# Attention and two MLPs on one core: the first chunk's output in two parts, and where weight conversions stand

## The chip, the cores and the metric

One core of a Trainium2 chip runs the whole program. The metric is the device time of one execution in microseconds; of the kernel before, three timed runs gave 955.28 to 957.27 with a median of 955.95.

## The reference

Attention with local and global queries, and then two MLPs, all in float32 (the weights arrive as float64):

```python
# q_l, k_l, v_l: (4, 8, 512, 64)   q_g, k_g, v_g: (4, 8, 32, 64)
k_all, v_all = concat([k_g, k_l]), concat([v_g, v_l])
out_g = softmax(q_g @ k_all.T / 8) @ v_all
s_ll  = where(abs(i - j) <= 32, q_l @ k_l.T / 8, -1e9)
out_l = softmax(concat([q_l @ k_g.T / 8, s_ll])) @ v_all
x = concat([out_g, out_l])  ->  (2176 tokens, 512)
h = x @ w_in;  x = max(0.01 h, h) @ w_out       # first MLP, 512 -> 2048 -> 512
h = x @ w2_in; out = (h - tanh(h)) @ w2_out     # second MLP, same sizes
```

## The kernel before

**Precision.** Every float32 matrix of an MLP is split into two parts (`hi` and `lo`, tiles of type F32R), and a product is three matmuls: hi*hi, lo*hi, hi*lo. Weights arrive as pairs of 32-bit words. `convert_w` (L117) makes float32 of them with one ScalarE step (L126) and three VectorE steps on integers (L127, L131, L134); `split_w` (L139) then makes hi on ScalarE and lo on VectorE. A conversion in this text is all six steps for one 128-wide slice of a weight matrix.

**Chunks and items.** The 2176 tokens are cut into five chunks of 512, 512, 512, 256 and 384 (the last with the 128 global tokens). The hidden size of 2048 is 16 slices f of 128. An item (phase, c, f) is one slice of one chunk. In phase 1 an item does `mlp1_a(c, f)`, 12 matmuls that make h, and the ScalarE and VectorE steps that make g, its hi part gh and its lo part gl; two items later (`SKEW`) `mlp1_b(c, f)` does 12 matmuls that add this slice's share to the chunk's y in four PSUM banks y0 to y3. After f = 15 `mlp1_y` (L226) copies the four banks out and stores them to `y_dram[c]`. All 16 slices of chunk 0 come first, then those of chunk 1, and so on; item number n = 16 c + f. Phase 2 is the second MLP, over the same chunks.

**Attention.** `stage(s)` (L762) returns up to five operations for one pair of heads and half a batch row (32 pairs): keys and queries of s + 1 by transposition (`kps`, `qps`), scores of s (`sps`) and their softmax, the output of s - 2 (`avps`) with the global scores (`sgps`), and the two transpositions of the probabilities of s - 1 (`ptps`). Global queries add `gtps`, `gt2ps` and `gavps` now and then. A chunk can start when the stages that fill its x have run: stages up to 17 for chunk 1, 25 for chunk 2, 33 for chunks 3 and 4.

**Order.** Stages 0 to 9 (`PRE` = 10) run ahead of the first item, with seven PSUM banks to rotate through (`start_tags`, L752); later attention has three (`run_tags`), while h has one bank and y four. Then the table `beside` (L861 to L872) says which operations go with which item: stages 10 to 17 beside items 0 to 15, 18 to 25 beside 15 to 31, 26 to 33 beside 31 to 47. They are put between the item's eight steps. TensorE's order is as written for items 0 to 77 (`fix`, L820); the other engines' order, SP's queue of transfers among them, is made by the planner from a simulation and the order of the code.

**Weights of the first MLP.** `in_load` (L682) loads a slice of w_in, 512 KB; `in_job` (L699) converts it in place, and it stays. One load stands ahead of the stages, one in each of the ten stages, and one in each of the first items; one conversion stands in each of stages 2 to 9 (eight), the other eight in items 0 to 7. `out_job` converts a slice of w_out, in items 1 to 16, and stores both parts to DRAM; later chunks fetch them (`wo_fetch`, L154), two items ahead. A conversion of these is kept behind the latest exponential and the latest attention output in the code (`converted`, L693).

**Weights of the second MLP.** From item 22 to 44 `w2_job` (L725) converts the 32 slices and stores them to DRAM, through two buffers `wraw` for loads and two `wf` for converted tiles; chunk 4's items fetch them.

**Places of x.** `xh` and `xl` are two pairs of tiles, 512 and 640 tokens wide; `place` says where a chunk's x lies: chunk 0 in the first, chunk 1 in the second, chunk 2 in the first again, chunk 3 and 4 in the second.

Of the kernel before, what the change touches and what calls it, by code (L numbers as in the profile page):

```python
# [21 lines left out]
def kernel(  # L22
# [14 lines left out]
    nc = tc.nc  # L37
# [16 lines left out]
    def mm(o, lhsT, rhs, start, stop):  # L54
        nc.tensor.matmul(o, lhsT, rhs, start=start, stop=stop)  # L55
# [22 lines left out]
    xl = [persist.tile([128, ND, n], F32R, name=f"xl{n}") for n in (512, 640)]  # L78
    ident = persist.tile([128, 128], F32, name="ident")

    y_dram = [dram.tile([128, ND, 512], F32, name=f"yd{c}") for c in range(5)]
    wo_dram = [dram.tile([128, 2, DM], F32, name=f"wod{f}") for f in range(NF)]
    w2i_dram = [dram.tile([128, DM], F32, name=f"w2id{f}") for f in range(NF)]
# [5 lines left out]
    sizes[4] += B * SG  # L89
    order2 = [0, 1, 2, 4, 3]  # L90

    place = [(0, 0), (1, 0), (0, 0), (1, 0), (1, 256)]

    def f32(t):
        return t.bitcast(F32)
# [102 lines left out]
    def mlp1_g(c, f, h):  # L198
# [6 lines left out]
        anchor[0] = nc.vector.tensor_sub(gl[:, :N], g[:, :N], f32(gh)[:, :N])  # L205
        g_t[c, f] = gh, gl

    def mlp1_b(c, f):
        N = sizes[c]
        gh, gl = g_t.pop((c, f))  # L210
        if f == 0:
            for d in range(ND):
                y_ps[d] = bank(f"y{d}", f"y{d}")
        hi, lo = wo_t.pop(f)

        def part(d):
            ds = slice(d * 128, (d + 1) * 128)
            mm(y_ps[d][:, :N], hi[:, ds], gh[:, :N], f == 0, False)
            mm(y_ps[d][:, :N], lo[:, ds], gh[:, :N], False, False)
            mm(y_ps[d][:, :N], hi[:, ds], gl[:, :N], False, f == NF - 1)  # L220
            if d == ND - 1:
                mlp1_y(c, f)

        return [lambda d=d: part(d) for d in range(ND)]

    def mlp1_y(c, f):  # L226
        N = sizes[c]
        if f == NF - 1:
            for d in range(ND):
                st = mlp.tile([128, 512], F32, tag="yst", name="yst", bufs=2)  # L230
                if d % 2:
                    nc.scalar.activation(st[:, :N], y_ps[d][:, :N], AF.Copy)
                else:
                    nc.vector.tensor_copy(st[:, :N], y_ps[d][:, :N])
                nc.sync.dma_start(out=y_dram[c][:, d, :N], in_=st[:, :N])


    att_ctx = ExitStack()
# [443 lines left out]
    def in_load():  # L682
        if in_todo:
            f = in_todo.pop(0)
            place = persist.tile([128, DM, 2], I32, tag=f"win{f}", name=f"inraw{f}")
            in_raw.append((f, load_w("in", w1_in, f, place)))
# [60 lines left out]
        tc.cur_priority = at + max(tc.cur_priority - max(at - n, 0), 0)  # L747

    gtodo = []
    w2_first = 22  # L750

    start_tags = ["att0", "att1", "att2", "y0", "y1", "y2", "y3"]  # L752
    run_tags = ["att0", "att1", "att2"]
# [74 lines left out]
    if True:  # L828
# [16 lines left out]
        for pp in range(PRE):  # L845
            for op in stage(pp):
                op()
            in_load()
            if pp == 0:
                load_kq(2)  # L850
            if pp == 1:
                load_v(1)
            if pp >= 2:
                in_job()
            if pp == PRE - 2:
                out_load()
                out_load()
        tags[0] = run_tags


        beside = {}  # L861
        pp = PRE
        n0 = 0
        for c, n1 in enumerate((NF - 1, 2 * NF - 1, 4 * NF - 16)):
            last = (starts[c + 1] + sizes[c + 1]) // HALF * NP + 1 if c < 2 else NU // 2 + 1
            ops = []
            while pp <= last:
                ops += stage(pp)
                pp += 1
            for k, op in enumerate(ops):  # L870
                beside.setdefault(n0 + k * (n1 - n0) // len(ops), []).append(op)
            n0 = n1  # L872
        items = [(1, c, f) for c in range(5) for f in range(NF)] + [(2, c, f) for c in order2 for f in range(NF)]

        n1 = 5 * NF
        for k in range(2):
            items.insert(n1 - 2 + 1 + 2 * k, items.pop(n1 + k))
        w2_at = {}
        for k in range(2 * NF + 1):
            w2_at.setdefault(w2_first + k * (44 - w2_first) // (2 * NF), []).append(k)  # L880
        last0 = 9 * NF
        b_at = {}
        for n, (ph, c, f) in enumerate(items):
# [2 lines left out]
        for n in range(len(items) + 8):  # L886
            ph, c, f = items[n] if n < len(items) else (3, 0, 0)
            one = items[n - 1] if 0 < n <= len(items) else (3, 0, 0)
            if ph == 1:
                if c == 0:  # L890
                    in_load()
                    in_job()
                    if f > 0:
                        out_job()
                elif c == 4 and f == 0:
                    while gtodo:
                        gtodo.pop(0)()
                    att_ctx.close()
                    p2 = ctx.enter_context(tc.tile_pool(name="p2", bufs=1))
                    for k in range(NF - 1):  # L900
                        wo2_t.append([p2.tile([128, ND, 128], F32R, name=f"wo2{x}{k}") for x in "hl"])
                    wo2_t.append([x[1][:, :, 512:] for x in (xh, xl)])
                    x2_load(0, 0)
                    x2_load(0, 1)
                if c == 4 and 2 <= f < 2 + ND:
                    x2_split(0, f - 2)
            elif ph == 2 and order2.index(c) + 1 < 5:
                nx = order2[order2.index(c) + 1]
                if f in (2, 3):
                    x2_load(nx, f - 2)  # L910
                if 5 <= f < 5 + ND:
                    x2_split(nx, f - 5)
            if ph == 1 and NF - 2 <= c * NF + f < 5 * NF - 2:
                fetches.append((f + 2) % NF)
            if one[0] == 1 and one[1] == 0:
                if one[2] == NF - 1:
                    out_job()
            while fetches:
                wo_fetch(fetches.pop(0))
            ops = beside.pop(n, [])  # L920
            if ph == 2:
                mlp2_a(c, f)
            if ph == 3:
                while p_t:
                    mlp2_split()
            steps, last = [], []
            for k in b_at.get(n, []):
                p, c1, f1 = items[k]
                if p == 1:
                    steps += mlp1_b(c1, f1)  # L930
                else:
                    last.append((c1, f1))
            if ph == 1:
                steps = mlp1_a(c, f) + steps
            if ph == 1 and not ops and gtodo:
                ops = [gtodo.pop(0)]
            K, M = len(ops), len(steps)
            at = [int((i + 0.5) * M / K) for i in range(K)]
            for m, step in enumerate(steps):
                step()  # L940
                while at and at[0] <= m:
                    at.pop(0)
                    ops.pop(0)()
            for op in ops:
                op()
            for c1, f1 in last:
                mlp2_b(c1, f1)
            if ph == 1 and c == 4:
                w2_place("out", f, fetch2(w2o_dram[f]))
                w2_place("in", f, fetch2(w2i_dram[f]))  # L950
            if ph == 1:
                for _ in w2_at.get(n, []):
                    w2_job()
            fix(n + 1)
            stores()
# [30 lines left out]
```

## Time and profile before

| | |
|---|---|
| median of 3 timed runs | 955.95 us |
| profiled execution: its time, and its span | 951.37 us, 949.6 us |
| before the first item | 0 to 65.13 us |
| items 0 to 15, and 16 to 47 | 65.13 to 200.81, 200.81 to 450.72 us |
| items 48 to 79, and the second MLP | 450.72 to 563.17 us, to the end |
| busy, share of the span: TensorE, VectorE, ScalarE | 97%, 66%, 57% |
| moved by DMA | 127.11 MB, mean 134 GB/s |

Shares are means over parts of very different kind, so the table's last lines say little alone: in the second MLP TensorE works without a gap, while ahead of the first item, and in the first of them, several engines wait for each other. A stretch begins where the first matmul that makes h of its first item starts. In the rows below PE is TensorE, DVE VectorE, ACT ScalarE, POOL GpSimd, SP the queue of transfers; line 55 is the helper through which all matmuls go, so products are told apart by the names of their tiles.

### The profile page before, as it was taken

The page shows a single profiled execution, that of the slowest core. Times are in us where ns is not written, and L with a number is a line of the kernel's source. Part 1 is how long each engine was busy: PE and PEld are TensorE (multiplying, and loading weights), DVE is VectorE, ACT ScalarE, POOL GpSimd, SP SyncE. Part 2 cuts the span into 40 slices and gives each one's busy share as a digit, 9 for nine tenths or more (in the row PEclk, how much of TensorE's full clock was granted, in tenths as well). Part 3 has the DMA queues.
Part 4 walks back from the last instruction along what each step waited for, and adds up shares of the span by engine and source line. Part 5 has one row for each costly group of instructions (what it writes and reads, how often), then busy time and mean ns, then how long its engine had stood idle before and what let it go on. Part 6 is the DMA issues. An engine that isn't in the chain of part 4 may idle for free.

```text
span 949.6 us, 15416 instructions
## 1 busy us (share of the span) xinstructions
PE 923.4 (97%) x5436; PEld 768.7 (81%) x5436; DVE 625.6 (66%) x1365; ACT 536.7 (57%) x1223; POOL 37.6 (4%) x67
## 2 busy tenths in 40 slices
PE   7788999999999999999999999999999999999998
PEld 5566778777777777778999998888888888899997
DVE  3988885633465555563213348878888887878886
ACT  5876676655465545454323447655656655555565
POOL 5310000000000000000000000000000000000022
PEclk9989999999999999999999999999999999999999
DMA  8897467575468877776656674001100100010010
GB/s 201 241 271 184 139 181 203 158 215 153 129 203 249 255 241 228 246 231 186 208 194 195 204 241 143 1 1 34 45 1 1 67 1 1 1 45 1 1 35 23
DMA packets 144941, 127.11 MB, mean 134 GB/s; under 512 B 89184, under 2 KB 107616, under 8 KB 144864
## 3 DMA queue, kind: packets, MB, share of 16 engines
q1 hardware_dynamic: 142208, 125.47, 43.7%
q8 instruction: 43, 0.70, 0.3%
q10 hardware_dynamic: 2656, 0.66, 0.3%
q14 instruction: 34, 0.28, 0.1%
HBM read 100.40 MB, written 25.69 MB: 133 GB/s over the span
## 4 chain that ended last, share of the span: by engine, by line
PE 86%; DMA 6%; ACT 3%; DVE 2%; SPq 1%; issue 1%; POOL 0%; ACTq 0%; DVEq 0%
PE h L55 37%; PE o L55 20%; PE y L55 18%; PE sps L55 3%; PE avps L55 2%; PE ptps L431 2%; DMA wraw<-in_moe_w_in_dram 1%; DMA wraw<-in_moe_w_out_dram 1%; PE sgps L55 1%; DMA w2od<-wf 1%; PE gavps L55 1%; ACT e L401 1%; PE kps L332 1%; ACT wf L126 1%; DMA w2id<-wf 1%
## 5 line engine op out<-in xcount | busy, mean ns | idle before, releaser
L55 PE MATMUL h<-xh,win 128*128 128x512 f32 (+2 forms) x1280 | 358.3, 363 | 1.1 <-ACT g L203 0.9
L55 PEld LDWEIGHTS h<-xh,win 128*128 128x128 f32 x1280 | 228.6, 189 | 34.9 <-issue 2.5
L55 PE MATMUL h<-xl,win 128*128 128x512 f32 (+2 forms) x640 | 230.5, 360 | 0.0
L55 PEld LDWEIGHTS h<-xl,win 128*128 128x128 f32 x640 | 121.1, 189 | 16.2
L205 DVE TENSOR_TENSOR gl<-g,gh 128x512 fp32r<-128x512 f32 (+2 forms) x80 | 48.8, 611 | 115.4 <-ACT gh L204 110.7
L55 PE MATMUL y<-gh,woh 128*128 128x512 f32 (+2 forms) x320 | 122.0, 381 | 0.0
L55 PE MATMUL y<-gh,wol 128*128 128x512 f32 (+2 forms) x320 | 115.2, 360 | 0.0
L55 PE MATMUL y<-gl,woh 128*128 128x512 f32 (+2 forms) x320 | 114.5, 361 | 0.0
L55 PE MATMUL o<-wo2l,gh 128*128 128x512 f32 x255 | 99.6, 391 | 0.0
L55 PE MATMUL o<-wo2h,gh 128*128 128x512 f32 x255 | 99.4, 390 | 0.0
L55 PE MATMUL o<-wo2h,gl 128*128 128x512 f32 x255 | 97.7, 390 | 0.0
L611 ACT ACTIVATE u<-h 128x512 f32<-128x512 f32 (+2 forms) x80 | 42.6, 532 | 93.1 <-PE h L55 86.2
L203 ACT ACTIVATE g<-h 128x512 f32<-128x512 f32 (+2 forms) x80 | 42.2, 528 | 56.3 <-PE h L55 55.7
L55 PEld LDWEIGHTS y<-gh,woh 128*128 128x128 f32 x320 | 60.6, 189 | 12.7 <-issue 6.7
L636 ACT ACTIVATE gh<-p 128x512 fp32r<-128x512 f32 (+2 forms) x80 | 45.4, 568 | 41.2 <-DVE p L620 40.4
L55 PEld LDWEIGHTS y<-gl,woh 128*128 128x128 f32 x320 | 60.7, 190 | 8.6
L126 ACT ACTIVATE wf<-wraw 128x512 f32<-128x512 f32 x48 | 31.7, 669 | 61.5 <-DMA w2od<-wf 15.2
L55 PEld LDWEIGHTS y<-gh,wol 128*128 128x128 f32 x320 | 61.0, 190 | 5.7
L617 ACT ACTIVATE u<-u,consts 128x512 f32<-128x512 f32 (+2 forms) x80 | 52.7, 659 | 6.8 <-DVE p L615 4.2
L637 DVE TENSOR_TENSOR gl<-p,gh 128x512 fp32r<-128x512 f32 (+1 forms) x64 | 41.9, 655 | 21.6 <-ACT gh L636 21.5
L55 PEld LDWEIGHTS o<-wo2h,gl 128*128 128x128 f32 x255 | 47.9, 188 | 10.2
L55 PEld LDWEIGHTS o<-wo2h,gh 128*128 128x128 f32 x255 | 48.0, 188 | 9.0
(107 smaller groups left out, 1426.6 us busy)
## 6 DMA issues: line engine op xcount, KB each, us to landing
wraw<-in_moe_w_out_dram SPq DMA_DIRECT2D x32, 512.0 KB, 4.6
woh<-wod SPq DMA_DIRECT2D x64, 256.0 KB, 3.6
wol<-wod SPq DMA_DIRECT2D x64, 256.0 KB, 3.2
inraw<-in_moe_w_in_dram SPq DMA_DIRECT2D x16, 512.0 KB, 5.9
wraw<-in_moe_w_in_dram SPq DMA_DIRECT2D x16, 512.0 KB, 5.0
vr<-in_v_l_dram SPq DMA_DIRECT2D x48, 96.0 KB, 3.0
kr<-in_k_l_dram SPq DMA_DIRECT2D x47, 96.0 KB, 2.9
vn<-in_v_l_dram SPq DMA_DIRECT2D x32, 128.0 KB, 3.7
```

Source lines behind the costliest of these rows:

```text
L55: nc.tensor.matmul(o, lhsT, rhs, start=start, stop=stop)
L126: nc.scalar.activation(w, hw.bitcast(F32), AF.Copy, scale=REBIAS)
L203: nc.scalar.activation(g[:, :N], h[:, :N], AF.Prelu, alpha=0.01)
L205: anchor[0] = nc.vector.tensor_sub(gl[:, :N], g[:, :N], f32(gh)[:, :N])
L332: nc.tensor.transpose(ps[:, c : c + n], kr[:n, t].rearrange("p h d -> p (h d)"), ident[:n, :n])
L401: last_exp[0] = nc.scalar.activation(e[:, h, j, s0 : s0 + n], x, AF.Exp, bias=st[:, k : k + 1], scale=-1.0, accum_out=st[:, 4 + k : 5 + k],)
L431: nc.tensor.transpose(ps[:, k * 128 : (k + 1) * 128], e[:, h, j, c0 : c0 + 128], ident)
L611: nc.scalar.activation(u, h, AF.Square)
L617: nc.scalar.activation(u, u, AF.Square, bias=tc_a2)
L636: nc.scalar.activation(gh[:, :N], p, AF.Copy)
L637: eng["pool" if i == order2[-1] else "dve"].tensor_sub(gl[:, :N], p, f32(gh)[:, :N])
```

## The change

The items of phase 1 come in another order: slices 0 to 7 of chunk 0 (n = 0 to 7), all of chunk 1 (8 to 23), slices 8 to 15 of chunk 0 (24 to 31), then chunks 2, 3 and 4 as before. The first half of chunk 0's y is evicted after its eighth slice and stored to a new DRAM tile `yp`; `y_part` loads it at item 32 into the half of chunk 0's x tiles that no one reads any more, and the eviction of the second half adds it (eight adds on VectorE, two for each bank). Chunk 2's x now lies in the second pair of tiles and chunk 3's in the first.

The stages move: 10 to 17 beside items 0 to 6, none beside 8 to 23, 18 to 25 beside 24 to 30, 26 to 29 beside 32 to 46, 30 to 33 beside 48 to 57. In the ten stages ahead of the items a load of w_in stands in every second one and a conversion in stages 2, 4, 6 and 8; four conversions stand in items 0, 2, 4 and 6 and eight in items 8 to 15. Conversions of w_out stand in items 1 to 8 and 17 to 24. The second MLP's conversions stand in items 25 to 47. The number of matmuls is the same.

```diff
+    yp_dram = dram.tile([128, ND, 512], F32, name="yp")
-    place = [(0, 0), (1, 0), (0, 0), (1, 0), (1, 256)]
+    place = [(0, 0), (1, 0), (1, 0), (0, 0), (1, 256)]
...
+    HF = NF // 2
+    def y_first(c, f):
+        return f // HF * HF if c == 0 else 0
+    def y_last(c, f):
+        return f // HF * HF + HF - 1 if c == 0 else NF - 1
+    def y_part():
+        for k, x in enumerate((xh[0], xl[0])):
+            nc.sync.dma_start(out=f32(x)[:, :, 256:], in_=yp_dram[:, :, 256 * k : 256 * k + 256])
...
-        if f == NF - 1:
+        if f == y_last(c, f):
             for d in range(ND):
                 st = mlp.tile([128, 512], F32, tag="yst", name="yst", bufs=2)
-                if d % 2:
+                if c == 0 and f == NF - 1:
+                    for k, x in enumerate((xh[0], xl[0])):
+                        ks = slice(256 * k, 256 * k + 256)
+                        nc.vector.tensor_add(st[:, ks], y_ps[d][:, ks], f32(x)[:, d, 256:])
+                elif d % 2:
                     nc.scalar.activation(st[:, :N], y_ps[d][:, :N], AF.Copy)
                 else:
                     nc.vector.tensor_copy(st[:, :N], y_ps[d][:, :N])
-                nc.sync.dma_start(out=y_dram[c][:, d, :N], in_=st[:, :N])
+                to = yp_dram if f < NF - 1 else y_dram[c]
+                nc.sync.dma_start(out=to[:, d, :N], in_=st[:, :N])
...
-    w2_first = 22
+    w2_first = 25
...
-            in_load()
+            if pp % 2 == 0:
+                in_load()
...
-            if pp >= 2:
+            if pp >= 2 and pp % 2 == 0:
                 in_job()
...
+        items = [(1, 0, f) for f in range(HF)] + [(1, 1, f) for f in range(NF)]
+        items += [(1, 0, f) for f in range(HF, NF)] + [(1, c, f) for c in (2, 3, 4) for f in range(NF)]
+        items1 = list(items)
+        items += [(2, c, f) for c in order2 for f in range(NF)]
...
-        for c, n1 in enumerate((NF - 1, 2 * NF - 1, 4 * NF - 16)):
-            last = (starts[c + 1] + sizes[c + 1]) // HALF * NP + 1 if c < 2 else NU // 2 + 1
+        for last, n0, n1 in ((17, 0, HF - 1), (25, 3 * HF, 4 * HF - 1), (29, 2 * NF, 3 * NF - 1), (NU // 2 + 1, 3 * NF, 4 * NF - 6)):
...
-            w2_at.setdefault(w2_first + k * (44 - w2_first) // (2 * NF), []).append(k)
+            w2_at.setdefault(w2_first + k * (47 - w2_first) // (2 * NF), []).append(k)
...
-                if c == 0:
+                if n in (0, 2, 4, 6) or HF <= n < 2 * HF:
+                    in_job()
+                if n < 2 * HF - 2:
                     in_load()
-                    in_job()
-                    if f > 0:
-                        out_job()
-                elif c == 4 and f == 0:
+                if 1 <= n <= HF or 2 * HF + 1 <= n <= 3 * HF:
+                    out_job()
+                if n == 4 * HF:
+                    y_part()
+                if c == 4 and f == 0:
...
-            if ph == 1 and NF - 2 <= c * NF + f < 5 * NF - 2:
-                fetches.append((f + 2) % NF)
+            if ph == 1 and HF <= n + 2 < 5 * NF and not 2 * HF <= n + 2 < 3 * HF:
+                fetches.append(items1[n + 2][2])
```

## Rows read from the trace of the kernel before

**Rows 1.** The page: busy time (share) xinstructions, VectorE's busy tenths in 40 slices.

```profile
PE 923.4 (97%) x5436; PEld 768.7 (81%) x5436; DVE 625.6 (66%) x1365; ACT 536.7 (57%) x1223; POOL 37.6 (4%) x67
...
DVE  3988885633465555563213348878888887878886
```

**Rows 2.** Chain of waits, second MLP: start us, us, what.

```profile
597.36 2.72 PE o L55 x12
```

**Rows 3.** Windows: stretch and its us, busy us (xinstructions) by engine, clock, DMA.

```profile
20.00:65.13 45.13, 37.58 (x369) 28.18 (x369) 41.04 (x84) 35.14 (x116) 14.99 (x14) 0.96 0.90 255
...
208.25:239.10 30.85, 30.85 (x181) 23.93 (x180) 10.47 (x37) 15.70 (x39) 0.30 (x2) 1.00 0.48 144
```

**Rows 4.** Chain of waits, before the first item.

```profile
22.72 1.42 DVE wt L131
...
45.40 5.94 DMA vr<-in_v_l_dram
```

**Rows 5.** Chain of waits, 265 to 393 us.

```profile
279.56 0.89 PE gavps L55 x20
...
320.75 5.97 DMA w2od<-wf
...
350.79 6.24 DMA wraw<-in_moe_w_in_dram
```

**Rows 6.** TensorE's timeline, before items: start us, us, instruction. Keys of a stage.

```profile
16.29 0.47 PE L332 MATMUL kps<-ident,kr 128*128 128x128 f32 x3
...
20.78 0.47 PE L332 MATMUL kps<-ident,kr 128*128 128x128 f32 x3
...
60.42 0.47 PE L332 MATMUL kps<-ident,kr 128*128 128x128 f32 x3
```

**Rows 7.** TensorE's timeline: first products of items 16, 17, 19, 31 and 40.

```profile
200.81 0.62 PE L55 MATMUL h<-xh,win 128*128 128x512 f32 x2
...
208.25 0.62 PE L55 MATMUL h<-xh,win 128*128 128x512 f32 x2
...
223.66 0.62 PE L55 MATMUL h<-xh,win 128*128 128x512 f32 x2
...
319.45 0.62 PE L55 MATMUL h<-xh,win 128*128 128x512 f32 x2
...
392.80 0.62 PE L55 MATMUL h<-xh,win 128*128 128x512 f32 x2
```

**Rows 8.** Windows, instructions on wt alone (three VectorE steps of a conversion).

```profile
20.00:65.13 45.13, 17.62 (x21) 0.96 0.90 255
...
95.49:134.39 38.90, 18.03 (x30) 1.00 0.51 153
```

**Rows 9.** Windows, instructions on win alone (a conversion's split; later also products).

```profile
20.00:65.13 45.13, 0.00 (x0) 0.04 (x1) 4.95 (x6) 3.81 (x6) 0.96 0.90 255
...
95.49:134.39 38.90, 15.93 (x60) 10.89 (x60) 3.44 (x5) 3.13 (x5) 1.00 0.51 153
```

**Rows 10.** TensorE's timeline, items 0 to 3; in brackets idle time before, and releaser.

```profile
65.13 0.70 PE L55 MATMUL h<-xh,win 128*128 128x512 f32 x2
...
68.97 0.61 PE L341 MATMUL qps<-ident,qr 128*128 128x128 f32 x2 [2.00 <-ACT pg L546]
...
84.75 0.44 PE L341 MATMUL qps<-ident,qr 128*128 128x128 f32 x2 [1.81 <-ACT pt L436]
...
95.49 0.62 PE L55 MATMUL h<-xh,win 128*128 128x512 f32 x2
```

**Rows 11.** Groups, 208.25 to 239.10 us: xcount | busy us, mean ns | idle before.

```profile
L205 DVE TENSOR_TENSOR gl<-g,gh 128x512 fp32r<-128x512 f32 x4 | 2.8, 692 | 13.7 <-ACT gh L204 13.7
...
L204 ACT ACTIVATE gh<-g 128x512 fp32r<-128x512 f32 x4 | 2.5, 631 | 0.1
...
L203 ACT ACTIVATE g<-h 128x512 f32<-128x512 f32 x4 | 2.4, 598 | 2.1 <-PE h L55 2.0
```

**Rows 12.** Tile yst (evictions of y): its stores' landing.

```profile
DMA to landing us min/median/max: 2.0/3.3/5.8
```

More of the change, by code (lines that the diff above doesn't have):

```diff
@@ L210, in mlp1_b @@
         gh, gl = g_t.pop((c, f))
-        if f == 0:
+        first, last = f == y_first(c, f), f == y_last(c, f)
+        if first:
             for d in range(ND):
@@ L217, in part @@
             ds = slice(d * 128, (d + 1) * 128)
-            mm(y_ps[d][:, :N], hi[:, ds], gh[:, :N], f == 0, False)
+            mm(y_ps[d][:, :N], hi[:, ds], gh[:, :N], first, False)
             mm(y_ps[d][:, :N], lo[:, ds], gh[:, :N], False, False)
-            mm(y_ps[d][:, :N], hi[:, ds], gl[:, :N], False, f == NF - 1)
+            mm(y_ps[d][:, :N], hi[:, ds], gl[:, :N], False, last)
             if d == ND - 1:
@@ L858 @@
         tags[0] = run_tags
+        items = [(1, 0, f) for f in range(HF)] + [(1, 1, f) for f in range(NF)]
+        items += [(1, 0, f) for f in range(HF, NF)] + [(1, c, f) for c in (2, 3, 4) for f in range(NF)]
+        items1 = list(items)
+        items += [(2, c, f) for c in order2 for f in range(NF)]
         beside = {}
         pp = PRE
-        n0 = 0
-        for c, n1 in enumerate((NF - 1, 2 * NF - 1, 4 * NF - 16)):
-            last = (starts[c + 1] + sizes[c + 1]) // HALF * NP + 1 if c < 2 else NU // 2 + 1
+        for last, n0, n1 in ((17, 0, HF - 1), (25, 3 * HF, 4 * HF - 1), (29, 2 * NF, 3 * NF - 1), (NU // 2 + 1, 3 * NF, 4 * NF - 6)):
             ops = []
@@ L871 @@
                 beside.setdefault(n0 + k * (n1 - n0) // len(ops), []).append(op)
-            n0 = n1
-        items = [(1, c, f) for c in range(5) for f in range(NF)] + [(2, c, f) for c in order2 for f in range(NF)]
         n1 = 5 * NF
@@ L912 @@
                     x2_split(nx, f - 5)
-            if ph == 1 and NF - 2 <= c * NF + f < 5 * NF - 2:
-                fetches.append((f + 2) % NF)
-            if one[0] == 1 and one[1] == 0:
-                if one[2] == NF - 1:
-                    out_job()
+            if ph == 1 and HF <= n + 2 < 5 * NF and not 2 * HF <= n + 2 < 3 * HF:
+                fetches.append(items1[n + 2][2])
             while fetches:
```

## The prediction

> **What bounds the kernel now.** Read the shares first [rows 1]: TensorE counts as busy 97% of the span. Matmuls of steady items follow each other every 0.227 us, 12 in 2.72 us [rows 2], so an item of 24 products is 5.44 us, and nothing in the change removes a matmul. What can be gained is time in which TensorE waits. So ask where that is: VectorE's row of the forty slices, 23.7 us each, stands at 8 to 9 tenths from the second to the sixth (24 to 142 us) and at 1 to 6 from there to 546 us [rows 1], and the windows give 41.04 us of VectorE in the 45.13 us before the first item, against 37.58 of TensorE and 35.14 of ScalarE [rows 3]. The chain of waits agrees: in this stretch it passes through a conversion's second VectorE step, 1.42 us [rows 4], as well as through the attention's own steps. After 95 us the chain is TensorE until the second layer's weights are converted, where it is held by loads and stores of 6 us [rows 5].
>
> The yardstick for a stage of attention: from the keys of one stage to those of the next TensorE needs 20.78 - 16.29 = 4.5 us when it doesn't wait [rows 6]; beside items it is the same, 223.66 - 208.25 = 15.41 for two items and one stage, less 10.88, which leaves 4.5 [rows 7]. The global queries add, per four stages, two sets of products at 0.89 us [rows 5] and a set of transposes that I put at 0.6 (an estimate), so 0.6 a stage: 5.1 in all.
>
> **Step A, the start.** Four of the eight conversions leave it. One costs VectorE 17.62 / 7 = 2.5 us for the three integer steps there [rows 8] and 4.95 / 6 = 0.8 for the split [rows 9], 3.3 in all, and ScalarE twice 3.81 / 6, 1.3 us [rows 9]. Without four, VectorE falls from 41.0 to 27.7 us, ScalarE from 35.1 to 29.8, and TensorE with 37.6 is the highest: it is late next. Seven stages now take 60.42 - 16.29 = 44.1 us, 6.3 each [rows 6]. If a stage with a conversion stays at 6.3 and one without falls to 5.1, seven stages save 7 x 0.6 = 4.2 us; if all fall to 5.1, 8.4 us. From below, nothing is saved if loads set the pace. I take 6.3, between the first two, since a conversion now has two stages to spread over. Five 512 KB loads also leave the code before the first item, and stand behind it in SP's queue, one per item; the loads of keys and values move up past them.
>
> **Step B, the first half of chunk 0.** Eight stages stood beside 16 items and now stand beside items 0 to 6; items 8 to 23 have none. Now the 16 items take 200.81 - 65.13 = 135.7 us [rows 7, 10]. TensorE's own work is 14 x 5.44 + 2 x 2.72 (the first two have no second half) + 8 x 5.1 = 122.4, so 13.3 us are waits. About 10 of them lie in items 0 to 2 (65.13 to 95.49, 30.4 us for 10.9 of products and some two stages [rows 10]): conversions stand on ScalarE and VectorE in front of the copies that free attention's PSUM banks, and TensorE waits 2.0 and 1.8 us for such copies [rows 10].
>
> In the new order a dense item has 8/7 of a stage: 5.44 + 5.8 = 11.3 us of TensorE, and 8.5 in the first two. ScalarE, from the window of two stages and four items: (15.70 - 2.4 - 2.5) / 2 = 5.4 a stage at most, so 6.2, plus 1.2 for g and gh, plus 1.5 conversions (10 or 11 in seven items, against two per item now) at 1.3: 9.4 us [rows 3, 9, 11]. VectorE by the same rows: (10.47 - 2.8) / 2 x 8/7 + 0.7 + 1.5 x 2.5 = 8.8, with a conversion at 18.03 / 10 + 3.44 / 5 = 2.5, since all its steps are shorter after 95 us [rows 3, 8, 9, 11]. So TensorE sets items 2 to 6, with cover of about 2 us, and ScalarE sets items 0 and 1. I charge 2 us for each of the first two, by the two waits above, and 0.6 for each of the next five, an estimate between nothing (the pair of items in [rows 7]) and 2.0. Items 7 to 15 wait for nothing, at 5.4 us with one conversion each. Sum 7 us against 13.3: a gain of 6.3. From both sides: 13.3 gained if no dense item waits, 14.7 lost over both dense groups together if every one waits 2 us (second rival).
>
> **Step C, the second half of chunk 0.** Items 24 to 30 are dense too, in place of stages at half that density that lost nothing visible [rows 7]. They carry 1.5 second-layer conversions each, which have one ScalarE step instead of two (0.65 us and not 1.3), so 8.4 us of ScalarE beside 11.3 of TensorE. I charge 0.4 each: 3 us lost; 0 to 14 by the same ends.
>
> **Step D, the second layer's conversions.** 33 jobs on 22 items, as before, but from item 25 instead of 22. In the 9 items 31 to 39, 319.45 to 392.80 us, 13 jobs pass now, one in 5.6 us, and the chain runs through their loads and stores [rows 5, 7]. Of the new order's jobs 22 fall on items 32 to 47, which have four stages instead of eight and last 16 x 5.44 + 4 x 5.1 = 107 us: one in 4.9 us. Weights and converted tiles have two buffers each. A buffer that is loaded in 6.2 us [rows 5] and converted in 0.6 + 1.8 = 2.4 [rows 8, 9] comes round in 8.6 us, 4.3 a job of two buffers, so the pace can be held, with little slack. Charge 3 us; ends: a gain of some 5 (what the chain's waits may cost there now) and a loss of 16 (first rival).
>
> **Step E, y in two parts.** Four more evictions, four stores and two loads of 512 KB, and eight adds in place of four copies. Between items 9 and 10, counted from item 9's start, banks are complete at 3.4, 4.1, 4.8 and 5.4 us; the third copy waits for the first store out of two buffers, 4.1 + 3.3 (median landing [rows 12]) + 0.7 = 8.1 us, and item 10 needs that bank at 9.5. So item 10's first half hides it with 1.4 us to spare; with the longest landing of 5.8 us [rows 12] it is 1.1 us late. The adds, half as wide as the subtraction that makes gl, take no more than its 0.69 us each [rows 11], and the loaded part has two items (12 us) to arrive. Behind SP's wait for item 31's reads stand weight fetches two items ahead of need. I charge 0.5; ends 0 and 3.
>
> **Sum.** -6.3 - 6.3 + 3 + 3 + 0.5 = -6.1 us. Against the profiled execution, 951.37 us (span 949.6), that gives 945.3. It ran 4.6 us below the median of the three timed runs, so the prediction is 955.95 - 6.1 = 949.9 us.
>
> **Rivals.** (1) *Slower: the second layer's ring is what paces items 32 to 47.* If 5.6 us a job is what loads, stores and SP's one queue can do, 22 jobs take 123 us instead of 107: +16 in place of +3, sum +7, 963 us. It decides from (107 + 3 + 6.1) / 22 = 5.3 us a job on. For it: the chain's pieces that are DMAs of 6 us [rows 5]. Against: the jobs' present pace is also simply what the item count sets. (2) *Slower: dense items.* Three PSUM banks serve attention beside items, seven in the start. If each of the 14 dense items waits 2 us for a bank, B and C become 28 - 13.3 = +14.7, sum +11.9, 968 us; no gain is left from 1.15 us an item on. For it: the two waits of [rows 10], both just after the banks became three. Against: those had two conversions per item, and only 2.7 us of products to hide them. The Trainium skill speaks for this one (Perfetto Trace Analysis, Optimization Strategy): of a kernel with several regimes it says that time may be won by interleaving them, and this change does the opposite, with 16 items bare of attention beside 14 full ones. By that rule the time would be this rival's 968 us; the trace has no item this dense, and so neither confirms nor denies it. (3) *Same: loads pace the start.* Then A is 1 and the sum -0.8: 955.2 us. For it: the chain waits 5.94 us for a load of values [rows 4]; against: VectorE's 91%. That the planner fills the freed time with the same conversions ends here too; but the code holds a conversion behind the latest exponential and output of attention. (4) *Better:* A 8.4, dense items lose 2 us in all, D and E nothing: -8.4 - 11 = -19.4, 936.5 us.
>
> **How the numbers follow.** Forecast 0.46 (own range 943 to 954), better 0.20, same 0.12, ring 0.12, dense items 0.10. What a measurement of this kernel can tell from no change is about 0.2%, 1.9 us. Faster: 0.46 + 0.20 + 0.04 of rival 3 = 0.70; within 0.10; slower 0.20, with some of rival 3 on either side. A range of 938 to 963 leaves out the dense items' case, half of the ring's dearer end and the far end of the better one, under 0.2 together.
>
> **What would show it.** A: the first matmul of h at 58 to 60 us instead of 65.13, VectorE near 60 to 70% before it. B: item 7 reached within 82 to 92 us of that, items 8 to 15 at 5.5 us each, and the h of item 16 some 12 us sooner than 200.81. C: items 24 to 30 at 11 to 12.5 us each; waits of TensorE for copies to attention's banks above 1 us a stage would be rival 2. D: items 32 to 47 in 107 to 113 us; 120 or more, with ScalarE waiting for w loads and stores, rival 1. E: no TensorE wait at items 10 and 34. The prediction is wrong if the start does not shorten, or if what it gains is lost in the dense items.

## The result, and the profile after

The changed kernel takes 965.73 us (median of 4 runs, 964.21 to 969.4), the kernel before 955.64 (955.28 to 957.27) on the same chip: a ratio of 1.0108, 95% interval 1.0077 to 1.0139. It is slower by 10.1 us where a gain of 6.1 was forecast, and outside the range. Its profiled execution took 965.56 us with a span of 963.8. That of the kernel before lay 4.3 us below its median, so the two profiles differ by more than the medians: 963.8 - 949.6 = 14.2 us of span. The account below is made in these 14.2.

The page after, parts 1 and 2, against [rows 1]:

```profile
PE 925.9 (96%) x5436; PEld 771.4 (80%) x5436; DVE 624.5 (65%) x1373; ACT 536.9 (56%) x1223; POOL 36.9 (4%) x67
...
DVE  3864878544564454555313347988888988888886
```

The busy times are those of before within 3 us. VectorE's stretch of 8 and 9 tenths is broken up (8, 6, 4, 8, 7, 8 from the second slice on): the load is more even, though not by much. What grew is idle time of TensorE, 949.6 - 923.4 = 26.2 us before and 37.9 after. The windows say where; a stretch less TensorE's busy time in it is what TensorE waited there. Cut at the first products of items 0, 1, 16, 24, 31 (32 for the row behind it), 48 and 64, the third row holding items 0 to 15 as a whole, after:

```profile
20.00:59.71 39.71, 35.82 (x369) 27.17 (x370) 31.62 (x72) 31.81 (x111) 14.28 (x14) 1.00 0.84 235
59.71:81.11 21.40, 12.72 (x103) 9.95 (x101) 10.20 (x33) 11.46 (x32) 0.00 (x0) 0.76 0.84 235
59.71:198.14 138.43, 128.07 (x834) 100.09 (x832) 90.79 (x247) 86.74 (x215) 0.30 (x2) 0.96 0.65 184
198.14:241.66 43.52, 43.52 (x194) 36.05 (x193) 21.22 (x33) 17.68 (x29) 0.00 (x0) 1.00 0.51 170
241.66:327.00 85.34, 79.79 (x560) 60.03 (x558) 45.51 (x164) 52.16 (x147) 0.31 (x2) 0.97 0.63 180
334.20:450.14 115.94, 109.19 (x573) 85.17 (x571) 63.03 (x155) 49.87 (x113) 0.30 (x2) 0.99 0.78 247
450.14:515.32 65.18, 64.58 (x592) 60.27 (x592) 22.08 (x67) 30.37 (x81) 0.00 (x0) 1.00 0.61 190
```

and the same items before:

```profile
65.13:76.40 11.27, 8.89 (x69) 6.16 (x69) 8.24 (x25) 7.94 (x22) 0.00 (x0) 0.85 0.85 209
65.13:200.81 135.68, 130.51 (x848) 100.50 (x847) 98.19 (x269) 92.02 (x231) 0.30 (x2) 0.97 0.65 184
200.81:263.25 62.44, 62.44 (x379) 48.51 (x378) 23.95 (x79) 30.72 (x75) 0.30 (x2) 1.00 0.51 146
263.25:319.45 56.20, 55.37 (x358) 43.97 (x357) 33.75 (x95) 31.65 (x81) 0.00 (x0) 1.00 0.80 240
326.58:450.72 124.14, 121.65 (x743) 95.36 (x742) 68.63 (x183) 62.60 (x151) 0.30 (x2) 0.99 0.72 226
450.72:501.99 51.27, 51.27 (x430) 49.62 (x429) 9.72 (x22) 15.97 (x40) 0.00 (x0) 1.00 0.60 200
```

Subtracting stretch by stretch (items 0 to 15 are 198.14 - 59.71 and 200.81 - 65.13, item 31 is what lies between the windows):

| stretch | before | after | difference | forecast |
|---|---|---|---|---|
| A: to the first product of h | 65.13 | 59.71 | -5.4 | -6.3 |
| B: items 0 to 15 | 135.68 | 138.43 | +2.7 | -6.3 |
| C: items 16 to 31 (four stages from 16-23 into 24-30) | 62.44 + 63.33 | 43.52 + 92.54 | +10.3 | +3 |
| D, E: items 32 to 63 (four stages from 32-47 into 48-63) | 124.14 + 51.27 | 115.94 + 65.18 | +5.7 | +3.5 |
| item 64 to the end | 447.61 | 448.48 | +0.9 | 0 |

Of the 14.2 us 11.7 are waiting of TensorE: 3.7 less in A, and in the rows below it 5.2, 4.7, 4.9 and 0.6 more. The other 2.5 are busy time: the products are the same in number, but the granted clock was lower in some of these stretches. The rows of B and C also differ in work: what the old order does of a ninth stage before item 16 comes after item 24 in the new one (848 products of TensorE against 834 in B).

**Item 0** alone takes 21.40 us, 10.1 more than before. TensorE's timeline there (start, duration, instruction, idle before and its releaser), and a window of the stretch at the lower clock:

```profile
59.71 0.71 PE L55 MATMUL h<-xh,win 128*128 128x512 f32 x2
...
63.50 0.44 PE L363 MATMUL qps<-ident,qr 128*128 128x128 f32 x2 [2.54 <-ACT pg L568]
...
70.19 2.05 PE L55 MATMUL avps<-pt,vr 128*64 128x128 f32 x16 [4.65 <-DMA vr<-in_v_g_dram]
...
75.48 0.42 PE L55 MATMUL gavps<-pg,vg 32*64 32x32 f32 x4 [1.49 <-DMA vg<-in_v_g_dram]
75.83 1.22 PE L55 MATMUL h<-xh,win 128*128 128x512 f32 x2
```
```profile
68.83:79.07 10.24, 7.39 (x52) 6.19 (x53) 3.79 (x10) 2.18 (x5) 0.00 (x0) 0.50 0.67 151
```

TensorE waits 4.65 us for the values of its own stage. In that wait the granted clock falls to 0.50, the lower of its two levels (1.2 GHz), and stays there for 10.24 us: the pair of products that takes 0.71 us at 59.71 takes 1.22 at 75.83. In experiment 2, where these two waits are gone and the clock stays at 1.00, the same 103 products of item 0 keep TensorE busy for 9.56 us instead of 12.72. So the stop costs 4.65 + 1.49 + 3.2 = 9.3 us. SP's own timeline says why the values are late; first after, then before:

```profile
50.66 3.84 SPq L113 DMA_DIRECT2D inraw<-in_moe_w_in_dram  x5
...
55.87 5.76 SPq L113 DMA_DIRECT2D inraw<-in_moe_w_in_dram  x5
61.72 1.22 SPq L315 DMA_DIRECT2D vr<-in_v_l_dram  x1
62.98 1.88 SPq L317 DMA_DIRECT2D vr<-in_v_g_dram  x1
```
```profile
54.58 6.42 SPq L112 DMA_DIRECT2D inraw<-in_moe_w_in_dram  x6
...
62.83 0.58 SPq L293 DMA_DIRECT2D vr<-in_v_l_dram  x1
```

The planner put the w_in loads, which in the code stand beside the items, ahead of the value load in either kernel, six before and ten after: issuing the last five takes 5.76 us. Before, the values' products came at 74.07 us, so the load at 62.83 was early enough. After, the load is issued at almost the same time, but its use has moved up by 8.4 us, to 65.68, as experiment 2 shows. The rows are TensorE's before, and after with the loads mended:

```profile
74.07 1.24 PE L55 MATMUL avps<-pt,vr 128*64 128x128 f32 x16
```
```profile
65.68 1.24 PE L55 MATMUL avps<-pt,vr 128*64 128x128 f32 x16
```

**Items 24 to 47.** The chain of waits after, in order of time:

```profile
286.56 5.11 DMA w2id<-wf
291.77 0.32 ACT wf L127
...
292.92 0.36 ACT kt L356
293.33 1.56 PE sps L55 x7
...
349.67 5.66 DMA w2od<-wf
```

A second-layer conversion waits on ScalarE for the store of its buffer, and the copy of the keys, for which TensorE waits (1.49 us), stands behind it in ScalarE's queue. The longest wait of TensorE in items 27 to 30 comes the same way. ScalarE's row and TensorE's:

```profile
319.38 0.68 ACT L127 ACTIVATE wf<-wraw 128x512 f32<-128x512 f32 x1 [3.92 <-DMA w2od<-wf]
```
```profile
325.16 1.12 PE L453 MATMUL ptps<-ident,e 128*128 128x128 f32 x4 [2.28 <-DVE xl L485]
```

Behind the conversion stands, among others, ScalarE's step that makes xh; VectorE's step that makes xl needs xh, and is the last to read the bank that TensorE waits for. At item 34, where the two parts of y are joined, the same thing catches VectorE. ScalarE's, VectorE's and TensorE's timelines there:

```profile
355.43 0.66 ACT L127 ACTIVATE wf<-wraw 128x512 f32<-128x512 f32 x1 [2.56 <-DMA w2od<-wf]
356.00 0.61 ACT L205 ACTIVATE gh<-g 128x512 fp32r<-128x512 f32 x1
```
```profile
356.64 0.69 DVE L206 TENSOR_TENSOR gl<-g,gh 128x512 fp32r<-128x512 f32 x1 [3.74 <-ACT gh L205]
...
357.59 0.42 DVE L251 TENSOR_TENSOR yst<-y,xh 128x256 f32<-128x256 f32 x1
```
```profile
358.48 0.47 PE L55 MATMUL y<-gh,woh 128*128 128x512 f32 x1 [3.73 <-DVE yst L251]
```

The conversion waits 2.56 us for a store, gh stands behind it, gl waits for gh, the add of a y bank stands behind gl, and TensorE waits 3.73 us for the bank.

### The profile page after: what moved, and what is told of

Read it like the earlier page. It is cut to its first block, busy times and chain, and to the rows that moved or that the text cites. A ratio compares the mean times of both kernels' runs of the same rounds, so it can differ in the third digit from the quotient of the medians.

```text
span 963.8 us, 15440 instructions
## 1 busy us (share of the span) xinstructions
PE 925.9 (96%) x5436; PEld 771.4 (80%) x5436; DVE 624.5 (65%) x1373; ACT 536.9 (56%) x1223; POOL 36.9 (4%) x67
## 4 chain that ended last, share of the span: by engine, by line
PE 77%; DMA 10%; ACT 4%; DVE 4%; SPq 2%; issue 2%; POOL 0%; ACTq 0%; DVEq 0%
PE h L55 34%; PE o L55 19%; PE y L55 14%; DMA wraw<-in_moe_w_in_dram 3%; PE sps L55 2%; PE ptps L453 2%; PE avps L55 2%; ACT e L423 2%; DMA w2id<-wf 2%; DMA wraw<-in_moe_w_out_dram 2%; PE gavps L55 1%; DMA w2od<-wf 1%; ACT wf L127 1%; PE sgps L55 1%; PE kps L354 1%
## 5 line engine op out<-in xcount | busy, mean ns | idle before, releaser
L55 PEld LDWEIGHTS o<-wo2h,gl 128*128 128x128 f32 x255 | 47.9, 188 | 10.1
```

## The experiments

Three causes were in question: the order of loads on SP's queue, the ring of second-layer jobs (load, convert, store), and the dense items themselves with their three PSUM banks. Each kernel's time is its median, and each ratio is to the kernel before on the same chip. Item times are read from the first products of h, as in [rows 7].

**1. The start alone, and all but the start.** The first kernel is the one before with these lines of the change only; the second is the changed kernel with them undone.

```diff
-            in_load()
+            if pp % 2 == 0:
+                in_load()
...
-            if pp >= 2:
+            if pp >= 2 and pp % 2 == 0:
                 in_job()
```

> The kernel before, with the halved start alone: loads of w_in in every second stage and conversions in stages 2, 4, 6, 8 of the start, the order of items as before. Theory of the loads (what the start gains is lost because loads of values keep their place in SP's queue behind loads of w_in): the first matmul of h comes some 5 us sooner than 65.13, as in the changed kernel (59.71), and since attention here stays at half a stage per item, the values are needed late enough: 950 to 953 us in all. Theory of the dense items (they alone lose the time, the start's gain is real): the same 950 to 953 us. Theory that conversions only move (what leaves the start returns in items 0 to 11 on ScalarE and VectorE): 955 to 958 us.

> The changed kernel with the start as before: eight conversions and ten loads of w_in in the ten stages; order of items, y in two parts and all else as changed. Theory of the loads: the first h comes at about 65 us as before, but the dense item 0 finds its values landed, as fewer loads stand in front of them late: item 0 falls from 21.4 to 10 to 13 us, so that the start's 5 us are paid back and more, 960 to 965 us. Theory of the dense items: the start's gain of 5.4 us is lost and item 0 stays as it is: 970 to 973 us.

The start alone: 950.92 us, ratio 0.9969 (0.9951 to 0.9987), as two of the theories had it. All but the start: 965.0, 1.0121 (1.0085 to 1.0156). The start alone brings the first h to 59.95 us, but item 0 then takes 17.47 us instead of 11.27, with TensorE waiting for vr and vg:

```profile
71.48 1.24 PE L55 MATMUL avps<-pt,vr 128*64 128x128 f32 x16 [2.75 <-DMA vr<-in_v_g_dram]
...
77.07 0.42 PE L55 MATMUL gavps<-pg,vg 32*64 32x32 f32 x4 [3.34 <-DMA vg<-in_v_g_dram]
```

At item 1 the whole gain is paid back (77.42 us against 76.40 before); at item 16 half of it is there again (198.32 against 200.81). In the changed kernel nothing is left of it: item 16 comes at 198.14 us with the halved start and at 198.49 without. But loads alone don't explain the second kernel. Its item 0 takes 15.58 us, where the theory of the loads expected 10 to 13 and that of the dense items no change: TensorE waits there 0.49 us for a load, and 4.8 for ScalarE and VectorE.

**2. The w_in loads behind the value loads.** Their issue beside items is tied behind the newest load of keys or values on SP; the order of products is unchanged. First on the changed kernel, then on the start alone.

```diff
-                queues[t].dma_start(out=dst[96:, t], in_=glob[b, hs].rearrange("h s d -> s h d"))
+                last_ld[0] = queues[t].dma_start(out=dst[96:, t], in_=glob[b, hs].rearrange("h s d -> s h d"))
...
-                    in_load()
+                    with tc.issue_after(last_ld[0].ins): in_load()
```

> The changed kernel, with each load of w_in that stands beside an item queued on SP behind the newest load of keys or values in the code; TensorE's order is the same. Theory of the loads: the wait of 4.65 us for values in item 0 and the 10 us at half clock behind it go; item 0 falls from 21.4 to about 11 us, and the whole to 953 to 957 us. Theory of the dense items: item 0 waits for ScalarE, VectorE and PSUM banks instead, and the whole stays within 962 to 968 us.

> The kernel before with the halved start and the w_in loads beside items behind the value loads; y in one part, the old order of items. Queue theory: item 0, 17.5 us with the halved start alone, falls to 12 to 13, and the time from 950.9 to 946 to 948. If the time lost there is made up later anyway (the start's work is only moved), item 0 falls but item 16 comes at the same time as with the halved start alone, 198 us, and the time stays at 951.

On the changed kernel: 957.16 us, 1.0023 (1.0006 to 1.0041). On the start alone: 943.15, 0.9901 (0.9888 to 0.9915). Item 0 falls from 21.40 to 12.09 and from 17.47 to 11.23 us, and no wait for values is left. Items 0 to 15 of the changed kernel:

```profile
59.92:189.19 129.27, 124.93 (x833) 97.39 (x831) 90.63 (x247) 86.29 (x215) 0.30 (x2) 1.00 0.72 208
```

That is 6.4 us under the 135.68 of before, as much as step B forecast once the queue has the order that it assumed, though not for its reason (see below). By the ratios the queue cost the changed kernel 0.85%, 8.1 us, and the start alone 0.68%, 6.5 us. The second kernel shows more: without any of the new order of items the start and the queue together give 1%, more than was expected of it (946 to 948 us). The two kernels differ by the rest of the change alone, and that costs 1.2% (1.0023 against 0.9901), 11.7 us.

**3. The second layer's ring.** The 33 jobs spread over items 25 to 58 instead of 25 to 47: on the changed kernel, then with the loads mended as well; last, with the loads mended, over items 17 to 58.

```diff
-            w2_at.setdefault(w2_first + k * (47 - w2_first) // (2 * NF), []).append(k)
+            w2_at.setdefault(w2_first + k * (58 - w2_first) // (2 * NF), []).append(k)
```

> The changed kernel with the second layer's 33 conversion jobs spread over items 25 to 58 instead of 25 to 47, one per item instead of 1.5. Theory of the ring (loads and stores of these jobs pace items 32 to 47, first rival of the prediction): items 32 to 47 fall from 115.9 to 105 to 109 us, items 28 to 30 by some us, and the eviction of y at item 34 no longer waits behind a job: the whole 953 to 958 us. Theory of the dense items: items 24 to 30 stay at 85 us and 32 to 47 above 112; the whole 963 to 967 us.

> The changed kernel with both edits: w_in loads behind the value loads, second-layer jobs over items 25 to 58 instead of 25 to 47. If queue and ring are two separate losses, the gains add: 965.7 - 8.6 - 6.2 = 951 us, items 0 to 15 at 131 us, items 24 to 30 at 80 us, 32 to 47 at 111. If the two edits repair one and the same loss (half-clock stretches after any long wait), less than 3 us come on top of either, 955 to 957. Item 34 still shows TensorE waiting 3 us for a store buffer of y, since a conversion still stands in front of the adds.

> The changed kernel with w_in loads behind the value loads and the second-layer jobs over items 17 to 58, so that half as many of them as in the changed kernel lie beside items 24 to 47. Ring theory: items 24 to 30 fall to 77 to 79 us and 32 to 47 to 107 to 109, and the time to 947 to 949. Rival, dense items (attention's own waits cost there): 24 to 30 stay at 80 and 32 to 47 at 111, time 951. Rival, collision: the jobs now meet the output-weight conversions of items 17 to 24, and items 16 to 24 lose up to 5 us; time 952 to 955.

Ring alone: 959.52 us, 1.0054 (1.0033 to 1.0075), less of a gain than the theory of the ring expected (953 to 958 us). With the loads: 951.41, 0.9973 (0.9958 to 0.9989). The gains add up, 8.1 and 5.2 us apart against 12.9 together, so they are two losses. From item 17: 966.5, 1.0149 (1.0129 to 1.0169), a collision, and worse than any theory said. The windows of items 27 to 30 give the dose. The first row is items 3 to 6 of the changed kernel, as many stages without second-layer jobs; then, each from its own kernel, items 27 to 30 as changed (9 jobs beside items 25 to 30), over 25 to 58 (6 jobs) and over 17 to 58 (4 jobs):

```profile
101.71:145.69 43.98, 43.30 (x328) 33.55 (x327) 34.11 (x107) 34.45 (x95) 0.00 (x0) 1.00 0.67 189
274.82:327.00 52.18, 46.63 (x328) 35.57 (x327) 28.18 (x99) 30.43 (x84) 0.00 (x0) 0.95 0.66 189
```
```profile
265.61:314.15 48.54, 44.28 (x328) 33.79 (x327) 24.80 (x93) 28.82 (x82) 0.00 (x0) 1.00 0.63 172
```
```profile
283.71:328.45 44.74, 43.62 (x327) 33.48 (x327) 23.41 (x90) 28.60 (x81) 0.00 (x0) 1.00 0.61 164
```

With the same products (x327 or x328) four dense items take 44.0 us without jobs and 44.7, 48.5 and 52.2 with 4, 6 and 9. Of the 52.2 some 2.4 are the clock, which stood at 0.50 from 294.11 and from 324.83 us on, for 3.41 us each; with 9 jobs and the loads mended, at a clock of 1.00, the four items take 49.8. TensorE waits 0.7 us in the row without jobs, and 1.1, 4.3 and 5.6 in those with 4, 6 and 9. VectorE and ScalarE are *less* busy in the slower rows than in the first, so it is not the amount of their work that delays TensorE, but waiting in their queues: the eight conversions that ScalarE begins in the first row wait for no transfer, the six in the row with 9 jobs wait 9.4 us together, the longest 3.92.

The kernel from item 17 loses elsewhere: its jobs meet the conversions of w_out, and TensorE waits in item 22 for one, after which the clock's mean over that item is 0.84 and it takes 10.9 us instead of 5.44:

```profile
229.59 0.80 PE L55 MATMUL y<-gh,woh 128*128 128x512 f32 x1 [3.46 <-ACT woh L141]
```
```profile
223.25:234.12 10.87, 7.41 (x25) 5.43 (x24) 6.58 (x11) 3.76 (x6) 0.00 (x0) 0.84 0.67 206
```

It loses more in items 24 to 26, which take 44.0 us instead of 33.2: TensorE waits there twice for VectorE's steps on the scores, 2.86 and 3.07 us. The first time VectorE waits 4.10 us for a conversion on ScalarE, which waits for a load; the second time its copy out of a bank of y waits 4.64 us for an earlier store of y. The clock then stands at 0.50 for 10.24 us in all. So the short row with 4 jobs has its price ahead of it, and what the dose shows rests on the other rows.

**4. Seven PSUM banks in items 0 and 1**, on the changed kernel with the loads mended; from item 2 on y needs four of them.

```diff
-        tags[0] = run_tags
...
+            tags[0] = run_tags if n >= 2 else start_tags
```

> The changed kernel with the w_in loads behind the value loads, and items 0 and 1 with the start's seven PSUM banks for attention instead of three. Banks (rival 2): the 2.5 us that the query scores of item 0 wait for the exponential of the global scores go, item 0 falls from 12.1 to 9.6 us, and the time from 957.2 to about 954.7. Engines, not banks: the copies are late themselves, item 0 stays within 0.7 us of 12.1 and the time within 1 us of 957.2. Items 2 to 6 keep their lengths in either case, since they have three banks in both kernels.

950.98 us, 0.9976 (0.9961 to 0.999), 4.5 us less than with three by the ratios, where 2.5 were expected; of them the profiles show 3.3 in items 0 to 15. The 2.5 us wait of the query transposes, [2.54 <-ACT pg] in the rows above, is gone, and item 0 falls from 12.09 to 9.46 us:

```profile
60.06:69.52 9.46, 9.42 (x104) 7.46 (x101) 8.05 (x30) 9.41 (x30) 0.00 (x0) 1.00 0.76 184
```

So banks do bind in the first two items, which have no y products, as [rows 10] hinted; items 2 to 6, with three banks, keep their length within 0.3 us (55.8 and 55.6).

**5. The same repairs in both orders.** All kernels here have the halved start, the loads mended and seven banks in items 0 and 1. The old order of items with the old jobs (22 to 44); the old order with jobs over 25 to 58; the new order with jobs over 25 to 58; and the new order with no job beside items 31 to 35, where y is joined:

```diff
+            n = w2_first + k * (54 - w2_first) // (2 * NF)
+            w2_at.setdefault(n if n < 31 else n + 5, []).append(k)
```

> The old order with the halved start, w_in loads behind value loads and seven PSUM banks in items 0 and 1, second-layer jobs as in the kernel before. Banks: item 0 falls from 11.2 to 8.7 us and the time from 943.2 to 940.6. Engines: item 0 stays within 0.7 us of 11.2 and the time at 943. Item 39 keeps its 12.9 us in either case.

> The order of items of the kernel before, y in one part, with all three repairs: halved start with w_in loads behind value loads, seven PSUM banks in items 0 and 1, second-layer jobs over items 25 to 58. From the 943.2 us of the first repair alone: the banks' 2.5 us at item 0 and the 4.3 us that item 39 loses to a conversion waiting for a store go, so 936 to 938 us. If the second layer's ring has slack in the old order and item 39's stop only moves, 940 to 941.

> The changed order with y in two parts and the same three repairs. If all that the changed kernel lost were queue, ring and banks, the split is worth its own saving and this kernel is no slower than the old order with the same repairs. If the moved stages cost beside items 48 to 63 what they saved before item 48, and the split adds its stops at items 10 and 34, this is 951.4 - 2.6 = 949 us, 11 to 13 us above the old order with the same repairs.

> The changed order with the three repairs, and no second-layer job beside items 31 to 35, where the two parts of y are added (the other jobs keep their density). If the stop at item 34 comes from the second-layer conversion that stands in front of the adds and from its transfers beside the stores of y, item 34 falls from 9.3 to 6.3 us or less and the time by 3 us, to 946. If it comes from the two store buffers of y alone, item 34 stays above 8 us and the time at 949.

| kernel | us | ratio (95%) | items 0-15 | 16-23 | 24-31 | 32-47 | 48-63 | 64-86 |
|---|---|---|---|---|---|---|---|---|
| old order, old jobs | 939.02 | 0.9840 (0.9814-0.9866) | 127.08 | 62.44 | 63.75 | 124.71 | 51.27 | 94.29 |
| old order, jobs to 58 | 943.58 | 0.9891 (0.9864-0.9917) | 127.09 | 62.45 | 62.25 | 119.18 | 54.55 | 100.18 |
| new order, jobs to 58 | 946.8 | 0.9925 (0.9895-0.9955) | 125.67 | 43.52 | 87.84 | 110.88 | 69.23 | 96.51 |
| new order, none at the join | 946.3 | 0.9921 (0.9896-0.9947) | 125.69 | 43.52 | 87.55 | 105.95 | 71.63 | 95.95 |

The old order with the old jobs is the fastest kernel of the study, 1.6% under the one before; the banks took 4.3 us off its item 0 (11.23 to 6.90) where 2.5 were expected: the wait of 2.55 us, and 1.8 us of busy time (8.68 to 6.90), since the clock over the item, 0.85 with the wait, is 1.00 without it. Taking the jobs from the join lets item 34 fall from 10.02 to 5.93 us:

```profile
331.58:337.51 5.93, 5.93 (x29) 4.89 (x28) 1.71 (x4) 1.72 (x3) 0.00 (x0) 1.00 0.69 224
```

So the stop there was the ring's, not that of the two store buffers. But the time hardly follows, 946.3 us against 946.8 with overlapping intervals: the jobs pushed later cost 2.4 us more in items 48 to 63. Stretching the jobs in the old order missed its forecast (936 to 941 us) in the same way: it saves 7.1 us up to item 48 (its first product comes at 430.74 instead of 437.88) and loses more after. Items 48 to 63 and 64 to 86, first with the jobs stretched, then with the old jobs:

```profile
430.74:485.29 54.55, 51.97 (x431) 49.78 (x430) 25.68 (x51) 20.83 (x49) 0.00 (x0) 1.00 0.91 314
485.29:585.47 100.18, 96.20 (x518) 89.59 (x517) 52.84 (x89) 52.09 (x98) 0.00 (x0) 1.00 0.64 210
```
```profile
437.88:489.15 51.27, 51.27 (x431) 49.62 (x429) 9.73 (x22) 15.98 (x40) 0.00 (x0) 1.00 0.62 201
489.15:583.44 94.29, 94.29 (x518) 89.84 (x517) 49.21 (x84) 48.59 (x93) 0.00 (x0) 1.00 0.60 191
```

The late jobs fill the DMA engines (0.91 against 0.62), and the second layer's weights, read back from item 64 on, come late: TensorE waits 4.0 us in items 64 to 86, and nothing with the old jobs.

Does the new order have a worth of its own, with the losses mended that were found? In none of these runs. With the loads mended and seven banks, and the jobs that either kernel had, it is slower by 1.4% (0.9976 against 0.9840); with the jobs over 25 to 58 in both by 3.2 us, where 11 to 13 were expected, with intervals that overlap. The table's last row less its first, two kernels that differ in their jobs too, gives, stretch by stretch: -1.4, -18.9, +23.8, -18.8, +20.4, +1.7. Even the 1.4 us of items 0 to 15 are not won. First the old order's window there, then the new one's:

```profile
59.90:186.98 127.08, 126.24 (x849) 98.58 (x846) 103.27 (x280) 95.07 (x237) 0.31 (x2) 1.00 0.77 225
```
```profile
59.67:185.36 125.69, 123.96 (x833) 97.08 (x831) 90.47 (x247) 85.67 (x215) 0.30 (x2) 1.00 0.73 213
```

The new order does 2.3 us of work less there, which comes after item 24, and waits 0.9 us more. Four stages taken out of 16 to 23 cost 4.9 us *more* in 24 to 31: 2.5 of them are work so moved, 2.4 are waits. The four moved behind item 48 are lighter ones, with one set of keys and two of scores left among them, and cost 1.6 us more there than they save in 32 to 47. Over items 0 to 86 TensorE waits 11.7 us in the new order and 4.4 in the old one, more than the whole 6.7 us between the two profiles there.

## Why the prediction was wrong

**A held.** The first h came 5.4 us earlier against 6.3. Of these 3.7 are waits; 1.8 are shorter work, the same 369 products at a mean clock of 1.00 instead of 0.96, which the sum did not have. VectorE's share before it is higher than forecast, 31.6 of 39.7 us, 80% and not 60 to 70%, because three conversions left this stretch and not four: of the 21 steps on wt [rows 8] 12 are left, all on wt alone:

```profile
20.00:59.71 39.71, 9.62 (x12) 1.00 0.84 235
```

The gain is nearly whole all the same: TensorE, with 35.8 of 39.7 us, is now the busiest, as the sum had it. (The sum's 29.8 us of ScalarE should be 30.1 by its own rows; nothing hangs on it.)

**B failed, at a sentence that stands with step A: "the loads of keys and values move up past them".** It was read from the code, where the w_in loads now stand after the start. In the trace the planner had put six of them ahead of the value load already before, and it put ten there after; the sum never asked when that load was issued and how much sooner it would be needed. That cost 9.2 us in items 0 to 15 (138.43 against 129.27 with the loads mended), more than the forecast gain.

With the loads mended B comes out at 6.4 us against 6.3, but that is luck. The sum took as waits what was left of 135.7 us after an estimate of the work, 13.3 us, and forecast that 7 of them would stay. The window before shows 135.68 - 130.51 = 5.2 us of waiting, all of it in items 0 to 2, and 4.3 stay with the loads mended. The other 5.6 us are shorter work: some 2.3 are the part of the ninth stage that now comes after item 24 (experiment 5), the rest is the clock, 0.97 before and 1.00 with the loads mended. The parts offset each other too: items 2 to 6 took 55.8 us against 59.5 in the sum, items 7 to 15 took 52.6 against 49.0. Items 2 to 6 wait 0.7 us in all, and the charge of 2 us each for items 0 and 1 fits; most of it is the banks' share, which took 3.3 us off the two.

**C and D failed in size, and on the same omission.** The charge of 0.4 us an item counted ScalarE's work beside TensorE's, 8.4 against 11.3 us, as if its queue were free to go on. In the trace a conversion that waits on ScalarE for a load or a store, 1.7 to 3.9 us in items 27 to 30, holds the copies that stand behind it. The chain of [rows 5] showed these loads and stores, and the sum priced them only for items 32 to 47. Of C's 10.3 us, 8.2 lie in items 27 to 30, 52.2 us against 44.0 for the same products without jobs, where 3 were charged for all seven items; 4.9 of the 8.2 are waits, the rest is longer work, most of it at the lower clock. C's 10.3 also hold some 2.6 us of work that came over from items 0 to 15, which the sum for C left out. Items 32 to 47 took 115.9 us against 110; with the slower ring 110.9, and 106 with none at the join.

**E was mis-sized**: 0.5 forecast, and item 34 alone cost 4.1 (10.02 against 5.93). The working followed banks and stores at items 9 and 10 and took the adds at their own length; it did not ask what stands ahead of an add on VectorE, which is gl, behind gh, behind a conversion waiting for DMA. At item 10, too, TensorE waited 0.99 us for a copy out of a bank of y that waited for a store; the working had 1.1 us as its far end there and took none.

**The rivals.** The slower one with dense items named 968 us, the nearest figure, but not for its reason: it charged 2 us for banks to each of 14 dense items, and items 2 to 6, as dense as any, waited 0.7 us in all. In items 27 to 30 two of TensorE's waits, 1.32 and 2.28 us, are indeed for a bank that VectorE's xl has yet to read, but behind a conversion that waits for a transfer. No run gave these items more banks. The Trainium skill's advice behind this rival (Perfetto Trace Analysis, Optimization Strategy), that interleaving regimes may win time, fits the runs as far as they go: with the same repairs the order that spreads the stages was never the slower one, and with the old jobs it was the faster by 1.4%. That interleaving is the reason is not shown. The ring rival was right in kind and too narrow in place: it looked at items 32 to 47 alone and set 123 us there.

**What stays open.** With all repairs and no job at the join TensorE still waits 3.5 us in items 24 to 31 and 5.3 in 48 to 63, where the old order with the old jobs waits 1.1 and nothing. Before item 48 the waits follow the jobs (experiment 3), but no run had items 24 to 31 without them. Whether the new order with no second-layer job at all before item 48 would beat 939 us was not tried; the late loss of the stretched jobs speaks against it.

## What to carry to other kernels

When a change makes one engine ready earlier, list the loads that its next steps need, with the time at which the trace shows each *issued*, not where the code has it; a load that was hidden by a few microseconds turns into a wait, and the gain is paid back there. Read what there is to gain as a stretch less the engine's busy time in it (5.2 us in items 0 to 15), not as the stretch less an estimate of the work (13.3). When work is packed more densely, look in the engines' queues for an instruction that waits for a transfer in front of a copy that the dense part needs: busy shares don't show it. And try the cheap half of a change alone: here the halved start with two small repairs, without the split, gave 1.6%.

## What the runs showed that was not expected

One wait of 4.65 us cost more than itself: the granted clock went to 0.50 in it and stayed there for 10.24 us, and the work of item 0 took 3.2 us longer. The same stop with 2.75 and 3.34 us of waiting, in the start alone, made item 0 6.2 us longer than with the loads mended. The number of banks is worth 2.6 us at item 0 in the new order, as much as the wait that it removes, and 4.3 in the old one, where the clock rises as well. And spreading the ring's jobs over more items in the old order moved their cost instead of removing it: 7.1 us were won before item 48, more was lost after it, and the DMA share in items 48 to 63 went from 0.62 to 0.91.
